# An earlier load of the second full block's list entries, and fixed places for the products of the inverses, in an attention and two expert layers on one core

## The chip, the cores and the metric

One Trainium2 chip (trn2), one of its eight cores. The core has five engines that run their own streams of instructions: TensorE (PE; its weight loads are PEld), VectorE (DVE), ScalarE (ACT), GpSimd (POOL) and SyncE (SP), which here only issues DMAs. They wait for each other through semaphores. An engine also waits on its own semaphore where an instruction reads or overwrites what an earlier one of the same engine wrote or read.

The metric is the time of one execution on the device in microseconds. Before the change three runs took 1020.48, 1023.16 and 1031.33 us, median 1023.16 us.

## The reference

Attention is a recurrence over 768 tokens for 4 x 8 heads of size 40. Its output is 3072 rows of 320 numbers. Two expert layers follow, each sending every row to the one of eight experts with the largest logit:

```
for t in range(S):                                   # S = 768, state 40 x 40 for each head
    y[t]  = r[t] @ state
    Sa    = state @ a[t]
    state = state * w[t] - outer(Sa, b[t]) + outer(v[t], k[t])
x = y as 3072 rows of 320
for layer in (1, 2):                                 # 8 experts, 320 -> 1024 -> 320
    e  = argmax(x @ w_gate (+ modality_bias[modality_id] in layer 2))
    out = softmax weight of e * (relu(x @ w1[e]) @ w2[e])   # rows of expert e only
    x  = out
```

## The kernel before

**Attention** works on 24 chunks of 32 tokens, all 32 heads together, four chunks to a group (groups 0 to 5). Within a chunk the recurrence is written as products of matrices. Its one sequential part is the inverse of a unit lower triangular 32 x 32 matrix for each head and chunk. The four chunks of a group are inverted together: 128 partitions hold one row set each, the matrix in `am`, the growing inverse in `tm` (both are parts of `z_sol` in the trace). `solve` does it by VectorE for groups 2 to 5, in 31 steps s = 0 to 30. Step s forms the product of column s of `am` below the diagonal with row s of `tm` into a scratch tile `pr` (`t1`, line 389), and takes it off the rows of `tm` below s (`t2`, line 395). A step with 64 or more elements and at least two rows is cut by `halves` into two pieces of rows; its four instructions then stand in the order product, product, difference, difference. That holds for steps 2 to 28. Groups 0 and 1 go by the class `Halves`: two 16 x 16 inverses side by side and a join. Its method `rest` (lines 479, 482) finishes the same matrix for the other three chunks, in the same pattern of steps.

The order of all work is written out by hand: `attention` calls the parts of a chunk one after another, and a list of small jobs (`Fill`) is drained between them at set fractions. The steps of the inverses are such jobs, and so are the decay products (lines 201 to 226). On each engine the instructions run in that order. Per chunk the state passes TensorE (`zps`, line 549), VectorE (`zs`, lines 555, 557) and TensorE again (line 523). VectorE also makes `z_ak` (line 363), the attention output `x` (line 1654) and the small steps of routing (lines 965 to 996) there.

**The experts** work on blocks of rows of one expert. `a0` and `b0` are blocks of 228 rows that the layer starts with, `b1` is the first block of 456 rows, and `bs[1]` the second. For a block, `entries` (lines 1238 to 1244) loads its list entries `le`: for each row its place in `x` and its weight. `load1` and `load2` (lines 1198 to 1208) load the first and second weights of its expert into `s1` and `s2`; `conv1` and `conv2` split them into two parts on ScalarE and VectorE. `gather` (line 1249) lets GpSimd fetch the rows that the entries name into `xg`; `split_x` (line 1263) transposes them on TensorE. `block(b, prev, nxt)` runs block b and prepares nxt. It starts with `entries(nxt)` and `load1(nxt)`, and puts `gather(nxt)` behind the first piece of layer 1, `load2(nxt)` behind the last, and the transposes of nxt between the pieces of layer 2. `put` (line 1361) scatters a finished block into `x`. Layer 1 reads its rows from the same `x`, so a gather waits for the last block's scatters. For `b0` the call is `block(b0, a0, b1, begun=True)`: entries, first load and gather of `b1` have been issued ahead of it.

All DMAs of SyncE are issued from one queue in order: an issue that waits holds those behind it.

Of the kernel before, what the change touches and what calls it, by code (L numbers as in the profile page):

```python
# [11 lines left out]
F32 = mybir.dt.float32  # L12
# [4 lines left out]
P = 128  # L17
# [16 lines left out]
FOLD = 18  # L34
FOLDS = (0, 0, 12, 24, 30)
PRES = (0, 0, 7, 15, 15)
TAIL, SPREAD, AHEAD = 42, 60, (80, 91)
WMID, WHALF = 1.4, 0.95
NG = NCH // 4
# [15 lines left out]
def attention(tc, zones, ident, r, k, v, w, a, b, emit_x, hook0, hook1, hook2, hook3, unsafe, extra, tail):  # L55
    nc = tc.nc
    with ExitStack() as ctx:
        cp = ctx.enter_context(tc.tile_pool(name="a_const", bufs=1))
        wp = ctx.enter_context(tc.tile_pool(name="a_work", bufs=2))
# [7 lines left out]
        cut = lambda z, at, *shape: view(zones[z], at, *shape)  # L67
# [300 lines left out]
        def solve(st):  # L368
            box = {}

            def t0():
                box["am"] = am = cut("sol", 0, L, L)
                box["tm"] = tm = cut("sol", L * L, L, L)
                nc.scalar.copy(tm, gtl[:, 3:4].unsqueeze(2).to_broadcast([P, L, L]))
                nc.scalar.copy(tm.rearrange("p t s -> p (t s)")[:, 0 : L * L : L + 1], gtl[:, 2:3].to_broadcast([P, L]))
                nc.vector.transpose(out=am, in_=st["aa"].rearrange("p h c t -> p t (h c)"))

            def halves(s):
                n = L - 1 - s
                if n < 2 or n * (s + 1) < 64:  # L380
                    return [(s + 1, L)]
                return [(s + 1, s + 1 + n // 2), (s + 1 + n // 2, L)]

            def t1(s, a, z):
                am, tm = box["am"], box["tm"]
                if a == s + 1:
                    box["pr"] = wp.tile([P, 256], F32, name="pr", bufs=1)
                prv = box["pr"][:, (a - s - 1) * (s + 1) : (z - s - 1) * (s + 1)].rearrange("p (t j) -> p t j", j=s + 1)
                nc.vector.tensor_mul(prv, am[:, a:z, s : s + 1].to_broadcast([P, z - a, s + 1]),  # L389
                                     tm[:, s : s + 1, : s + 1].to_broadcast([P, z - a, s + 1]))  # L390

            def t2(s, a, z):
                tm = box["tm"]
                prv = box["pr"][:, (a - s - 1) * (s + 1) : (z - s - 1) * (s + 1)].rearrange("p (t j) -> p t j", j=s + 1)
                nc.vector.tensor_sub(tm[:, a:z, : s + 1], tm[:, a:z, : s + 1], prv)

            def t3():
                st["tt"] = tt = wp.tile([P, L, 32], F32, name="tt")
                nc.vector.transpose(out=tt.rearrange("p t u -> p (t u)"), in_=box["tm"].rearrange("p t s -> p (t s)"))

            ops = [t0]
            for s in range(L - 1):
                for f in (t1, t2):
                    for a, z in halves(s):
                        ops.append(lambda f=f, s=s, a=a, z=z: f(s, a, z))
            return ops + [t3]

        class Halves:
# [10 lines left out]
            def ops(self):  # L419
                am, tm, st, n = self.am, self.tm, self.st, L // 2  # L420

                def t0():
                    self.pr = wp.tile([P, 256], F32, name="pr", bufs=1)
                    for o in (0, n):
                        nc.vector.transpose(out=am[:, o : o + n], in_=st["aa"].rearrange("p h c t -> p t (h c)")[:, o : o + n])

                def part(o, s):
                    return self.pr[:, 8 * o : 8 * o + (n - 1 - s) * (s + 1)].rearrange("p (t j) -> p t j", j=s + 1)

                def t1(o, s):  # L430
                    nc.vector.tensor_mul(part(o, s), am[:, o + s + 1 : o + n, o + s : o + s + 1].to_broadcast([P, n - 1 - s, s + 1]),
                                         tm[:, o + s : o + s + 1, o : o + s + 1].to_broadcast([P, n - 1 - s, s + 1]))

                def t2(o, s):
                    x = tm[:, o + s + 1 : o + n, o : o + s + 1]
                    nc.vector.tensor_sub(x, x, part(o, s))

                def t3():
                    self.rows = am[:, :n]
                    st["tt"] = tt = wp.tile([P, L, 32], F32, name="tt")  # L440
                    nc.vector.transpose(out=self.rows, in_=tm.rearrange("p t s -> p s t")[:, :n])
                    for o in (n, 0):
                        nc.vector.transpose(out=tt[:, o : o + n].rearrange("p t u -> p (t u)"), in_=tm[:, o : o + n].rearrange("p t s -> p (t s)"))

                ops = [t0]
                for s in range(n - 1):
                    for f in (t1, t2):
                        for o in (0, n):
                            ops.append(lambda f=f, o=o, s=s: f(o, s))
                return ops + [t3]  # L450
# [699 lines left out]
class Block:  # L1150
    def __init__(self, lay, tab, j, cut=None, first=False, ready=False, own=None):

        self.lay, self.tab, self.j, self.first, self.ready, self.own = lay, tab, j, first, ready, own
        self.cut, self.i = cut or lay.cut, None


class Rows:
# [23 lines left out]
class Experts:  # L1181
# [56 lines left out]
    def entries(self, b):  # L1238
        nc, c = self.nc, b.cut
        self.place(b)  # L1240
        r = nc.values_load(b.tab["reg"][0:1, 2, b.j : b.j + 1], engines=[ET.SP], min_val=0, max_val=LST - c.tb)
        d = nc.sync.dma_start(out=b.le, in_=b.lay.lst[ds(r, c.tb)].rearrange("(h p) w -> p h w", p=c.g))
        if self.loose and not b.lay.route:
            self.lrows.after(d.ins)
# [125 lines left out]
    def block(self, b, prev, nxt, hook=None, begun=False):  # L1370
# [12 lines left out]
                self.place(x)  # L1383
        if nxt is not None:
            if not begun:
                self.entries(nxt)
                self.load1(nxt)
                put(0, lambda: self.gather(nxt))
        for q in range(0 if b.ready else 4):
# [198 lines left out]
def network(tc, r, k, v, w, a, b, moe_w_gate, moe_w1, moe_w2, moe2_modality_id, moe2_w_gate, moe2_modality_bias, moe2_w1, moe2_w2, out):  # L1588
    nc = tc.nc
    with ExitStack() as ctx:  # L1590
# [30 lines left out]
        ex = Experts(tc, wt, ident, rt)  # L1621
# [113 lines left out]
        with ExitStack() as ctx2:  # L1735
# [44 lines left out]
            with tc.manual_schedule():  # L1780
                bs = [b1] + [Block(l1, b1.tab, j) for j in range(1, n1)]
                ex.loose = True
                ex.load1(b1)
                ex.gather(b1)
                for h in range(CUT0.h):
                    ex.put(a0, h)
                ex.block(b0, a0, b1, begun=True)
                prev = b0
                for b_, nxt in zip(bs, bs[1:]):
                    ex.block(b_, prev, nxt)  # L1790
                    prev = b_
                t2 = rt.ahead(tp, 1, CUT2, 2, counts(tp, 1))
                more = [Block(l2, t2, j, first=j == 0) for j in range(2)]
                ex.block(bs[-1], prev, more[0])
                tabs = []
                ex.block(more[0], bs[-1], more[1], lambda: tabs.append(rt.table(tp, 2, CUT2, counts(tp, 2), t2)))
                ex.run(more[1:] + [Block(l2, tabs[0], j) for j in range(n2)])
# [18 lines left out]
```

## Time and profile before

| what | value |
|---|---|
| median of three runs | 1023.16 us (1020.48 to 1031.33) |
| the profiled execution | 1024.33 us, its span 1022.1 us |
| TensorE busy | 906.4 us (89%) |
| VectorE busy | 706.1 us (69%) |
| ScalarE busy | 506.6 us (50%) |
| GpSimd busy | 304.7 us (30%) |
| mean granted clock of TensorE | 0.947 of full speed |

The shares are means over stages with different limits. Attention takes about the first half of the span, the experts the rest, where TensorE is busy for 464 of the 482 us after 540 us. What a row of a view means for one stage has to be read in that stage. The times in a timeline count from the start of the span. A row's idle time in brackets names what ended the wait; "issue" there stands for nothing that the profile shows. A row of a timeline may merge several instructions (x2); its length then runs from the first start to the last end.

### The profile page before, as it was taken

The page shows a single profiled execution, that of the slowest core. Times are in us where ns is not written, and L with a number is a line of the kernel's source. Part 1 is how long each engine was busy: PE and PEld are TensorE (multiplying, and loading weights), DVE is VectorE, ACT ScalarE, POOL GpSimd, SP SyncE. Part 2 cuts the span into 40 slices and gives each one's busy share as a digit, 9 for nine tenths or more (in the row PEclk, how much of TensorE's full clock was granted, in tenths as well). Part 3 has the DMA queues.
Part 4 walks back from the last instruction along what each step waited for, and adds up shares of the span by engine and source line. Part 5 has one row for each costly group of instructions (what it writes and reads, how often), then busy time and mean ns, then how long its engine had stood idle before and what let it go on. Part 6 is the DMA issues. An engine that isn't in the chain of part 4 may idle for free. (4 is left out here: it accounts for less than half of the span.)

```text
span 1022.1 us, 38222 instructions
## 1 busy us (share of the span) xinstructions
PE 906.4 (89%) x16089; PEld 838.8 (82%) x16089; DVE 706.1 (69%) x2022; ACT 506.6 (50%) x991; POOL 304.7 (30%) x361
## 2 busy tenths in 40 slices
PE   7747988788878888988879899999999999999995
PEld 7646777677767777766769799999999999999995
DVE  7799899998996985853545354545464776766762
ACT  6625445445445577643523254444443565665662
POOL 6550021211120211112133334543543433323321
PEclk9779979998999999998989899999999999999998
DMA  5554445433532623226017434445343111271110
GB/s 175 141 136 111 73 107 108 116 90 79 98 86 47 159 51 87 50 51 158 17 28 173 124 97 134 129 106 152 101 126 97 30 40 53 79 214 42 40 41 26
DMA packets 152421, 96.41 MB, mean 94 GB/s; under 512 B 127407, under 2 KB 139585, under 8 KB 151850
## 3 DMA queue, kind: packets, MB, share of 16 engines
q1 hardware_dynamic: 138154, 72.53, 28.3%
q0 software_dynamic: 14080, 21.28, 8.1%
q8 instruction: 130, 2.13, 0.9%
q14 instruction: 57, 0.47, 0.1%
HBM read 112.18 MB, written 14.59 MB: 124 GB/s over the span
## 5 line engine op out<-in xcount | busy, mean ns | idle before, releaser
L1293 PE MATMUL hp<-xs,h 128*128 128x256 f32 (+1 forms) x840 | 157.1, 317 | 0.0
L1304 PE MATMUL yp<-h,hh 128*114 128x320 f32 (+1 forms) x464 | 146.9, 317 | 0.3 <-DMA s<-moe_w 0.3
L1305 PE MATMUL yp<-l,hh 128*114 128x320 f32 (+1 forms) x464 | 144.2, 311 | 0.0
L1306 PE MATMUL yp<-h,hl 128*114 128x320 f32 (+1 forms) x464 | 144.0, 310 | 0.0
L1296 DVE SCALAR_TENSOR_TENSOR hl<-hp,hh 128x456 fp32r<-128x456 f32 (+1 forms) x116 | 76.6, 660 | 90.9 <-ACT hh L1295 90.9
L1293 PEld LDWEIGHTS hp<-xs,h 128*128 128x128 f32 x840 | 124.6, 190 | 3.3
L1295 ACT ACTIVATE hh<-hp 128x456 fp32r<-128x456 f32 (+1 forms) x116 | 66.5, 573 | 110.8 <-PE hp L1293 106.2
L1293 PE MATMUL hp<-xs,l 128*128 128x256 f32 (+1 forms) x504 | 102.5, 312 | 0.0
L1214 DVE TENSOR_TENSOR l<-s,h 128x768 fp32r<-128x768 f32 x88 | 80.6, 956 | 13.1 <-ACT h L1213 10.8
L1304 PEld LDWEIGHTS yp<-h,hh 128*114 128x114 f32 (+1 forms) x464 | 85.3, 184 | 0.6 <-issue 0.5
L1305 PEld LDWEIGHTS yp<-l,hh 128*114 128x114 f32 (+1 forms) x464 | 85.3, 184 | 0.2
L1306 PEld LDWEIGHTS yp<-h,hl 128*114 128x114 f32 (+1 forms) x464 | 85.1, 183 | 0.0
L1293 PEld LDWEIGHTS hp<-xs,l 128*128 128x128 f32 x504 | 80.1, 190 | 3.1
L1249 POOL DMA_INDIRECT xg<-x,le x52 | 61.9, 1190 | 69.2 <-issue 58.0
L1220 DVE TENSOR_TENSOR l<-s,h 128x640 fp32r<-128x640 f32 x88 | 72.6, 825 | 3.0 <-ACT h L1219 3.0
L1361 POOL DMA_INDIRECT out<-yo,ti x28 | 34.5, 1232 | 129.2 <-ACT yo L1357 74.7
L1213 ACT CAST h<-s 128x768 fp32r<-128x768 f32 x88 | 70.4, 835 | 1.6 <-DMA s<-moe_w 1.5
L1219 ACT CAST h<-s 128x640 fp32r<-128x640 f32 x88 | 63.3, 719 | 0.0
L389 DVE TENSOR_TENSOR pr<-z_sol 128x110 f32<-128x110 f32 (+20 forms) x232 | 58.5, 282 | 3.9
L985 POOL TENSOR_TENSOR ccnt<-ccnt,oh 128x8 bf16<-128x8 bf16 x24 | 6.7, 279 | 179.5 <-PE rp L983 145.7
L1003 POOL DMA_INDIRECT lst<-l2e,posi x32 | 40.8, 1276 | 60.9 <-DVE posi L996 53.5
L1267 DVE TENSOR_TENSOR xs<-ta,xs 128x456 fp32r<-128x456 f32 (+1 forms) x28 | 18.5, 662 | 55.2 <-ACT xs L1266 55.2
(364 smaller groups left out, 1996.2 us busy)
## 6 DMA issues: line engine op xcount, KB each, us to landing
s<-moe_w SPq DMA_DIRECT2D x22, 1280.0 KB
s<-moe_w SPq DMA_DIRECT2D x22, 1024.0 KB
s<-moe_w SPq DMA_DIRECT2D x44, 256.0 KB
z_w<-w SPq DMA_DIRECT2D x40, 160.0 KB
z_kb<-k SPq DMA_DIRECT2D x24, 160.0 KB
z_kb<-b SPq DMA_DIRECT2D x24, 160.0 KB
z_pa<-a SPq DMA_DIRECT2D x96, 40.0 KB
rt<-r SPq DMA_DIRECT2D x96, 40.0 KB
```

What stands on the lines that cost most here:

```text
L389: nc.vector.tensor_mul(prv, am[:, a:z, s : s + 1].to_broadcast([P, z - a, s + 1]), tm[:, s : s + 1, : s + 1].to_broadcast([P, z - a, s + 1]))
L1213: nc.scalar.copy(wt["h1"][:, :, s], wt["s1"][:, :, s])
L1214: nc.vector.tensor_sub(wt["l1"][:, :, s], wt["s1"][:, :, s], wt["h1"][:, :, s].bitcast(F32))
L1219: nc.scalar.copy(wt["h2"][:, s], wt["s2"][:, s])
L1220: nc.vector.tensor_sub(wt["l2"][:, s], wt["s2"][:, s], wt["h2"][:, s].bitcast(F32))
L1249: d = self.nc.gpsimd.indirect_dma_start(out=b.xg[:, h], out_offset=None, in_=b.lay.src, in_offset=IndirectOffsetOnAxis(ap=b.le[:, h, 0:1]. ...
L1293: nc.tensor.matmul(out=hp[:, i], lhsT=l, rhs=r, start=k == 0, stop=k == len(ops) - 1)
L1295: nc.scalar.activation(hh[:, s], hp, AF.Relu)
L1296: nc.vector.scalar_tensor_tensor(out=hl[:, s], in0=hp, scalar=0.0, in1=hh[:, s].bitcast(F32), op0=ALU.max, op1=ALU.subtract)
L1304: nc.tensor.matmul(out=yp, lhsT=hh[:, k, t], rhs=wt["h2"][:, k], start=k == 0, stop=False)
L1305: nc.tensor.matmul(out=yp, lhsT=hh[:, k, t], rhs=wt["l2"][:, k], start=False, stop=False)
L1306: nc.tensor.matmul(out=yp, lhsT=hl[:, k, t], rhs=wt["h2"][:, k], start=False, stop=k == 7)
```

## The change

Two things are done.

1. The products of an inverse get fixed places. Before, each step takes a new `pr` tile of 256 numbers (one buffer, so it lies where the last one lay), and the second half's product follows the first half's directly. Now one `pr` tile of 264 numbers is taken at the first step of an inverse; the first half's product, or that of a whole step, lies at 0, the second half's at 128. `Halves` takes the same tile of 264.
2. The list entries of `bs[1]` are loaded ahead of `block(b0, ...)`, and the call of `block` for `b1` doesn't load them again (`listed`).

```diff
+PR = 264
@@ solve
+            def place(s, a, z):
+
+                if "pr" not in box:
+                    box["pr"] = wp.tile([P, PR], F32, name="pr", bufs=1)
+                o = 128 if a > s + 1 else 0
+                return box["pr"][:, o : o + (z - a) * (s + 1)].rearrange("p (t j) -> p t j", j=s + 1)
+
             def t1(s, a, z):
                 am, tm = box["am"], box["tm"]
-                if a == s + 1:
-                    box["pr"] = wp.tile([P, 256], F32, name="pr", bufs=1)
-                prv = box["pr"][:, (a - s - 1) * (s + 1) : (z - s - 1) * (s + 1)].rearrange("p (t j) -> p t j", j=s + 1)
+                prv = place(s, a, z)
                 nc.vector.tensor_mul(prv, am[:, a:z, s : s + 1].to_broadcast([P, z - a, s + 1]),
                                      tm[:, s : s + 1, : s + 1].to_broadcast([P, z - a, s + 1]))
 
             def t2(s, a, z):
                 tm = box["tm"]
-                prv = box["pr"][:, (a - s - 1) * (s + 1) : (z - s - 1) * (s + 1)].rearrange("p (t j) -> p t j", j=s + 1)
+                prv = place(s, a, z)
                 nc.vector.tensor_sub(tm[:, a:z, : s + 1], tm[:, a:z, : s + 1], prv)
@@ class Halves, ops, t0
-                    self.pr = wp.tile([P, 256], F32, name="pr", bufs=1)
+                    self.pr = wp.tile([P, PR], F32, name="pr", bufs=1)
@@ class Block
-        self.cut, self.i = cut or lay.cut, None
+        self.cut, self.i, self.listed = cut or lay.cut, None, False
@@ class Experts, entries
         self.place(b)
+        b.listed = True
@@ class Experts, block
             if not begun:
-                self.entries(nxt)
+                if not nxt.listed:
+                    self.entries(nxt)
                 self.load1(nxt)
@@ network
                 for h in range(CUT0.h):
                     ex.put(a0, h)
+                ex.entries(bs[1])
                 ex.block(b0, a0, b1, begun=True)
```

On VectorE, in the first inverse that the change touches (steps 3 to 5 of group 2), the rows stood so before, with the semaphores that each waits for:

```order
L389 TENSOR_TENSOR pr<-z_sol 128x42 [waits DVE_49]
L389 TENSOR_TENSOR pr<-z_sol 128x45
L395 TENSOR_TENSOR z_sol<-z_sol,pr 128x14x3 [waits DVE_49]
L395 TENSOR_TENSOR z_sol<-z_sol,pr 128x15x3 [waits DVE_49]
L389 TENSOR_TENSOR pr<-z_sol 128x56 [waits DVE_49]
L389 TENSOR_TENSOR pr<-z_sol 128x56
L395 TENSOR_TENSOR z_sol<-z_sol,pr 128x14x4 [waits DVE_49] x2
L389 TENSOR_TENSOR pr<-z_sol 128x65 [waits DVE_49]
L389 TENSOR_TENSOR pr<-z_sol 128x70
```

and so they stand in the changed kernel, the same instructions in the same order:

```order
L395 TENSOR_TENSOR pr<-z_sol 128x42 [waits DVE_49]
L395 TENSOR_TENSOR pr<-z_sol 128x45
L401 TENSOR_TENSOR z_sol<-z_sol,pr 128x14x3 [waits DVE_49]
L401 TENSOR_TENSOR z_sol<-z_sol,pr 128x15x3 [waits DVE_49]
L395 TENSOR_TENSOR pr<-z_sol 128x56 [waits DVE_49] x2
L401 TENSOR_TENSOR z_sol<-z_sol,pr 128x14x4 [waits DVE_49] x2
L395 TENSOR_TENSOR pr<-z_sol 128x65 [waits DVE_49]
L395 TENSOR_TENSOR pr<-z_sol 128x70 [waits DVE_49]
```

Nothing moved; the second product of a step now has a wait of its own. The first product's wait is for another instruction than before: the last difference of the step ahead before (a new tile waits for all that used the old one), now the first difference, which read the place that it overwrites and wrote the row that it reads.

On SyncE, around `block(b0, ...)`, the rows before were these (`s_9408` and `s_9409` are the first and second weights, `le_14741` the entries of `bs[1]`):

```order
L1202 DMA s_9408<-moe_w 128x2x1024
L1204 ISA
L1204 DMA s_9408<-moe_w 64x1024
L1204 ISA
L1204 DMA s_9408<-moe_w 64x1024
L1208 ISA
L1208 DMA s_9409<-moe_w 128x8x320
L1241 TENSOR_LOAD small
L1241 ISA x2
L1242 ISA
L1242 DMA le_14741<-lst_61 114x4x4
```

and they are these in the changed kernel, where the buffers have other numbers:

```order
L1208 DMA s_9288<-moe_w 128x2x1024
L1210 ISA
L1210 DMA s_9288<-moe_w 64x1024
L1210 ISA
L1210 DMA s_9288<-moe_w 64x1024
L1248 TENSOR_LOAD small
L1248 ISA x2
L1249 ISA
L1249 DMA le_14621<-lst_61 114x4x4
L1214 ISA
L1214 DMA s_9289<-moe_w 128x8x320
```

The entries' DMA and the read of its register moved ahead of one DMA, the load of b1's second weights. GpSimd's gathers and scatters stand where they stood.

## Rows read from the trace of the kernel before

**Rows 1.** The profile's page, first line.

```profile
span 1022.1 us, 38222 instructions
```

**Rows 2.** Table by stretch: stretch, length; busy (instructions) of PE, PEld, DVE, ACT, POOL; granted clock.

```profile
184.00:238.00 54.00, 44.70 (x1297) 38.71 (x1298) 51.49 (x177) 21.59 (x49) 8.65 (x11) 0.87 0.39 95
...
249.00:296.00 47.00, 35.03 (x1181) 30.32 (x1180) 45.45 (x134) 20.06 (x45) 7.99 (x9) 0.96 0.52 111
...
345.00:440.00 95.00, 83.70 (x2845) 72.55 (x2846) 72.85 (x288) 63.26 (x137) 14.31 (x20) 0.98 0.37 76
579.00:586.00 7.00, 4.52 (x18) 4.52 (x18) 1.59 (x2) 1.70 (x3) 2.21 (x2) 0.51 0.20 39
```

**Rows 3.** TensorE's waits, 184 to 346 us: for what; total us, times, longest.

```profile
PE rp L982 <- DVE z_ak L363: 6.7, 5, 3.1
PE yps L592 <- DVE x L1654: 5.8, 4, 1.9
...
PE aab L358 <- DVE pr L389: 2.0, 1, 2.0
```

**Rows 4.** TensorE's waits, 346 to 440 us.

```profile
PE zps L549 <- issue: 4.3, 3, 2.4
```

**Rows 5.** VectorE's waits, 184 to 346 us.

```profile
DVE zs L555 <- PE zps L549: 2.7, 2, 2.1
```

**Rows 6.** VectorE's waits, 346 to 440 us.

```profile
DVE zs L555 <- PE zps L549: 5.6, 5, 2.9
```

**Rows 7.** VectorE's timeline, inverses of groups 2 and 5: start us, length us, instruction.

```profile
185.51 0.33 DVE L395 TENSOR_TENSOR z_sol<-z_sol,pr 128x42 f32<-128x42 f32 x2
185.87 0.35 DVE L389 TENSOR_TENSOR pr<-z_sol 128x56 f32<-128x56 f32 x2
186.14 0.34 DVE L395 TENSOR_TENSOR z_sol<-z_sol,pr 128x56 f32<-128x56 f32 x2
186.51 0.37 DVE L389 TENSOR_TENSOR pr<-z_sol 128x65 f32<-128x65 f32 x2
...
436.71 0.22 DVE L389 TENSOR_TENSOR pr<-z_sol 128x60 f32<-128x60 f32 x1
```

**Rows 8.** TensorE's timeline, transposes of bs[1]'s rows.

```profile
581.48 0.45 PE L1263 MATMUL ta<-ident,xg 114*128 114x114 f32 x1 [4.60 <-DMA xg<-x,le]
```

**Rows 9.** GpSimd's timeline, the first gather of bs[1].

```profile
568.07 1.21 POOL L1249 DMA_INDIRECT xg<-x,le x1 [8.14 <-issue]
```

**Rows 10.** Line 1361, 556 to 560 us: who waited for b0's scatter; its landing.

```profile
  POOL xg L1249: 8.1, 1
...
DMA to landing us min/median/max: 8.4/8.6/8.8
```

**Rows 11.** VectorE's timeline, second half of group 1's inverse, fixed places.

```profile
154.73 0.48 DVE L482 TENSOR_TENSOR z_sol<-z_sol,pr 128x128 f32<-128x128 f32 x2
155.13 0.47 DVE L479 TENSOR_TENSOR pr<-z_sol 128x112 f32<-128x112 f32 x2
```

**Rows 12.** Line 389 over the span: count, duration ns min/median/max, first and last start.

```profile
L389 DVE TENSOR_TENSOR pr<-z_sol x232: 158/262/1545, 184.3 to 437.2; 128x110 f32<-128x110 f32 x12, 128x120 f32<-128x120 f32 x12, 128x56 f32<-128x56 f32 x8, 128x78 f32<-128x78 f32 x8
```

**Rows 13.** TensorE's timeline, 232 to 239 us.

```profile
232.11 1.93 PE L358 MATMUL aab<-ab,kT 128*32 128x64 f32 x64 [2.68 <-ACT ab L339]
...
238.32 0.17 PE L982 MATMUL rp<-oh,tri 128*128 128x8 bf16 x1 [0.18 <-DVE z_ak L363]
```

**Rows 14.** ScalarE's timeline, ahead of that copy.

```profile
230.65 0.21 ACT L967 ACTIVATE ex<-dl 128x8 f32<-128x8 f32 x1 [4.51 <-DVE dl L966]
```

**Rows 15.** SyncE's issues around block b0: start us, length us.

```profile
541.18 0.47 SPq L1208 DMA_DIRECT2D s<-moe_w  x1
542.81 0.63 SPq L1242 DMA_DIRECT2D le<-lst  x1
```

**Rows 16.** Line 1242, 542 to 544 us: its waits, ns min/median/max.

```profile
L1242 SPq EVENT_SEMAPHORE  x5: 17/28/28, 542.4 to 542.7; - x5
```

**Rows 17.** ScalarE's timeline, first conversion of b1's second weights.

```profile
559.85 0.72 ACT L1219 CAST h<-s 128x640 fp32r<-128x640 f32 x1
```

## The prediction

> **What bounds the kernel now.** I read the table by stretch first, then the waits of TensorE, then VectorE's timeline inside the inverses, and last the queues around the first blocks of experts.
>
> The profiled execution took 1024.33 us, of which 1022.1 us are its span [rows 1]; the median of the three runs is 1023.16 us, 1.2 us below it. Both parts of the change sit in places of their own, so the table by stretch comes first [rows 2]. From 184 to 238 us VectorE is busy for 51.49 of 54 us, from 249 to 296 us for 45.45 of 47, while TensorE idles 9 and 12 us. From 345 to 440 us it is the other way: TensorE 83.70 of 95 us, VectorE 72.85. All four inverses of groups 2 to 5 run between 184 and 437 us.
>
> Who waits for whom says the same. Between 184 and 346 us TensorE waits for VectorE: 6.7 us for `z_ak`, 5.8 us for `x`, 2.0 us for a product of an inverse itself [rows 3], 14.5 us in these three rows. After 346 us no wait of TensorE names VectorE; the longest, 4.3 us before `zps`, ended by nothing the profile shows [rows 4]. VectorE's waits for `zps` tell which of the two was late at the hand-over of the state: two waits in the first stretch (2.7 us) [rows 5], five in the second (5.6 us) [rows 6]. So VectorE sets the pace up to about 345 us, TensorE after it.
>
> Inside an inverse a step is product, product, difference, difference. The reader is to add start and length of each row [rows 7]. The pair of products at 185.87 ends at 186.22, and the differences that wait for them begin at 186.14: 0.08 us before the end, because each waits for the product one further back. The pair of differences ends at 186.48; the next step's product begins at 186.51, 0.03 us after. It waits for the row directly ahead of it. One such joint thus costs 0.03 + 0.08 = 0.11 us.
>
> In the experts the place of the change is the hand-over from block b0 to b1 to the second full block (bs[1]). TensorE idles 4.60 us before 581.48 us for bs[1]'s gathered rows [rows 8]. The first gather was issued at 568.07 after 8.14 us of idle [rows 9], and that wait was ended by b0's scatter into `x`, which took 8.4 to 8.8 us to land [rows 10].
>
> **The change, part by part.** *Fixed places.* Before, a step's first product gets a new `pr` tile, so it waits for the last difference of the step before, which is the row directly ahead. With fixed places it waits for the difference of its own half, one row further back (that difference also made the row of the inverse it reads). That is the distance at which the differences already overlap by 0.08 us. There is also a row of the trace with the new form: the second half of group 1's inverse keeps its products at fixed places, and there the differences at 154.73 end at 155.21 while the next step's product starts at 155.13, again 0.08 us before [rows 11]. I take 0.11 us for each joint removed; the ends are 0 (the wait is paid anyway) and 0.11.
>
> How many? The 232 products [rows 12] are four inverses of 58: 27 steps in two halves and 4 whole ones. 27 steps of each inverse follow a step with two differences, 108 joints. In VectorE's timeline 93 of them start 0.03 us after the row ahead, the first at 185.87, the last at 436.71 [rows 7]; in the other 15 another job stands between and hides the joint. So VectorE's time falls by at most 93 x 0.11 = 10.2 us.
>
> Not all lies on the path. From 345 us on there are 45 joints; TensorE sets the pace there and does not wait for VectorE [rows 2, 4], so I cost their 5 us at nothing; TensorE's own chain hides them. Of the 48 earlier ones, three lie ahead of a wait of VectorE for `zps` [rows 5]. From 188 to 238 us there are 20, but TensorE's row at 238.32 had waited only 0.18 us for VectorE, and its run up to there began at 232.11 behind a copy of ScalarE that followed VectorE's routing step at 230.45 [rows 13, 14]; only the 15 joints before that move it. From 249 to 296 us there are 13, from 301 to 315 us three, from 325 to 345 us four; the remaining five fall where TensorE runs by itself. On the path: 15 + 13 + 3 + 4 = 35 joints, 35 x 0.11 = 3.9 us.
>
> *Added waits.* The second product of a step now waits too, for the second difference of the step before, with one product between. That is again the distance that shows 0.08 us of overlap [rows 7], so nothing. If that cover failed, 108 x 0.11 = 11.9 us would come back on VectorE and eat the gain. The tile grows by 8 words and is taken once for each inverse: nothing.
>
> *The list entries.* On SyncE's queue the entries of bs[1] go ahead of the load of b1's second weights instead of behind it. Before, the two were issued at 541.18 and 542.81 [rows 15], so they change places: the entries start some 1.6 us earlier and the weights 1.6 us later. The entries' DMA waits for semaphores, with that load and then the load of the next first weights queued behind it on SyncE; its waits in the trace took 17 to 28 ns each [rows 16], so they had been met. Gain: the gather that reads the entries was held by b0's scatter, not by them [rows 9, 10], so 0; the other end is the whole stall of 4.60 us [rows 8]. Loss: the weights were there when ScalarE's first conversion of them began at 559.85 with no idle ahead of it [rows 17]; 1.6 us later they delay it by 0 to 1.6 us. They were issued 18.7 us before that use, so I take 0. What is late next at bs[1] is what was late before: b0's scatter and then the gather.
>
> Sum: 1024.33 - 3.9 - 0 = 1020.4 us for an execution like the profiled one, and 1.2 us less against the median of the runs: **1019.2 us**.
>
> A rule speaks against this. The Trainium skill, VectorE: DVE Perf Modes, section The DRAIN you can't avoid, says that the next operation does not start until the pipeline is empty, and that eight copies took 13.88 us with a semaphore after each or only after the last. By it the sum would be 1024.33. The rows at 186.14 and 155.13 do not agree with it [rows 7, 11]: they begin before the row ahead ends.
>
> **The rivals.** *Handed back.* VectorE finishes sooner and waits for `zps`, `lp` or `yps`. For it: TensorE has gaps that nothing in the profile explains, also before 345 us, and VectorE does wait at times [rows 5]. Against it: 14.5 us of waits for VectorE [rows 3]. Time: 1023.2 us. 15%.
>
> *A joint costs its 0.11 us also without a wait on the row ahead* (the engine empties between jobs, and what I read as overlap is only how ends are recorded). Then nothing is saved: 1023.2 us. The starts themselves speak against it: 0.27 us from a step's first product to its first difference, 0.37 from there to the next step's product, on equal sizes [rows 7]. This is what the Trainium skill's section would give. 4%.
>
> *The entries do gate the gather.* If their landing was as late as the scatter's, the stall of 4.60 us goes, and with it the half clock behind it (0.51 over 7 us [rows 2], 3.4 us): 1019.2 - 8.0 = 1011.2 us. Against it: the wait is put down to the scatter [rows 10]. 6%.
>
> *The clock helps.* Over 184 to 238 us the granted clock is 0.87 [rows 2], so a quarter of the stretch ran at 1.2 GHz, behind gaps in which TensorE waited. Shorter gaps may keep it at 2.4 GHz; half of the 7 us lost there would give 1015.7 us. 13%.
>
> *Slower: the clock falls where TensorE sets the pace.* From 345 to 440 us the grant is 0.98. The gaps there are TensorE's own, and the change shifts everything by some us against transfers and against the clock's changes. Were the stretch granted the 0.87 of 184 to 238 us, TensorE would lose 0.11 x 95 = 10.5 us, and the end would be 1019.2 + 10.5 = 1029.7 us. It decides once more than 3.9 us are lost so. Against it: none of TensorE's gaps there names VectorE [rows 4], so none should grow. 6%.
>
> **How the numbers follow.** The forecast has 56%, for 1017.5 to 1021 us by itself. The range goes down to the clock's help with a little more, 1014.5 us, and up past no change (1023.2) by most of the weights' 1.6 us, 1024.5 us; what is left out is the entries' case and the slower one, and the tails. A measurement of this kernel can tell about 1% from no change, 1012.9 and 1033.4 us here. Faster by more than that needs the entries' case or nearly all 10.2 us: 6%. Slower by more needs the clock's fall and bad luck beside it: 3%. Within 1%: 91%.
>
> **What would show it.** In the inverses no product should start after the end of a difference directly ahead of it, save at the whole steps; VectorE's busy time from 184 to 345 us should fall, and the last inverse end some 4 us or more earlier. The waits of TensorE for `z_ak`, `x` and `pr` should shrink by about 4 us in all. The entries of bs[1] should be issued near 541 us less the shift, the weights behind them, and the gather should still wait for b0's scatter with a stall near 4.6 us. I am wrong if that stall goes, if the saved time turns up as longer waits of VectorE for `zps`, or if the stretch after 345 us becomes longer or shorter than before.

## The result and the profile after

Over 20 runs of each, the changed kernel takes 1010.79 us at the median (999.39 to 1021.25) and the kernel before 1020.36 us (1009.64 to 1031.33). The ratio is 0.9885, with a 95% interval of 0.986 to 0.991, so 9 to 14 us less. (It leaves out the longest runs of both kernels, so it is not quite the ratio of the medians, 0.9906.) The forecast was 1019.2 us. Of the 8.4 us between forecast and result, 2.8 are the base: the three runs shown had a median of 1023.16 us, twenty have 1020.36 us. The other 5.6 us are a gain that the prediction did not see.

The profiled execution took 1012.19 us. The first lines of its page answer to [rows 1]:

```profile
span 1010.0 us, 38222 instructions
PE 901.4 (89%) x16089; PEld 835.4 (83%) x16089; DVE 696.3 (69%) x2022; ACT 507.0 (50%) x991; POOL 305.1 (30%) x361
```

Its table by stretch (columns as in [rows 2], whose stretches it answers to; the last row is new):

```profile
184.00:238.00 54.00, 45.52 (x1419) 39.16 (x1423) 52.23 (x186) 23.39 (x53) 12.61 (x13) 0.94 0.41 98
249.00:296.00 47.00, 37.30 (x1207) 32.04 (x1207) 44.80 (x151) 20.24 (x45) 8.21 (x11) 0.89 0.45 97
341.00:435.00 94.00, 83.71 (x2776) 73.41 (x2776) 66.98 (x277) 61.89 (x133) 14.30 (x20) 0.95 0.39 80
554.00:584.00 30.00, 29.05 (x185) 27.50 (x184) 16.21 (x36) 13.38 (x26) 11.63 (x10) 1.00 0.46 134
```

The same 30 us around the hand-over to bs[1] stood so in the kernel before, some 6 us later in the span:

```profile
560.00:590.00 30.00, 25.40 (x146) 24.00 (x145) 13.19 (x29) 10.50 (x21) 8.98 (x8) 0.89 0.43 125
```

Two places gave the time. VectorE's busy time over the span fell from 706.1 to 696.3 us, and in this pair of traces the last step of an inverse came 5.7 us earlier (next but one fence). One pair does not give the size: in a second trace of each kernel (before_again and change_again, below) that step comes at 433.5 and 431.5 us, 2.0 us apart. And in the 30 us of the hand-over TensorE was busy for 3.7 us more, at full instead of 0.89 of its clock. After that nothing moves any more: the two traces run in parallel, the changed one 11.1 to 12.1 us ahead.

VectorE's timeline in the inverse of group 2, to lay beside [rows 7]:

```profile
186.11 0.34 DVE L395 TENSOR_TENSOR pr<-z_sol 128x56 f32<-128x56 f32 x2
186.37 0.34 DVE L401 TENSOR_TENSOR z_sol<-z_sol,pr 128x56 f32<-128x56 f32 x2
186.62 0.36 DVE L395 TENSOR_TENSOR pr<-z_sol 128x65 f32<-128x65 f32 x2
```

The differences of 186.37 end at 186.71, and the next step's product starts at 186.62, 0.09 us before that end. From product to product the step takes 0.51 us; before it took 0.64 [rows 7]. The joint was worth 0.13 us here; the prediction had 0.11.

The products over the span (columns as in [rows 12]):

```profile
L395 DVE TENSOR_TENSOR pr<-z_sol x232: 172/259/1601, 184.6 to 431.5; 128x110 f32<-128x110 f32 x12, 128x120 f32<-128x120 f32 x12, 128x56 f32<-128x56 f32 x8, 128x78 f32<-128x78 f32 x8
```

At the hand-over, the timeline of GpSimd, SyncE and TensorE in the changed kernel (L1368 is the scatter, L1256 the gather, L1214 the load of second weights):

```profile
537.34 0.32 SPq L1249 DMA_DIRECT2D le<-lst  x1
538.02 0.83 SPq L1214 DMA_DIRECT2D s<-moe_w  x1
...
552.41 0.39 SPq L1208 DMA_DIRECT2D s<-moe_w  x1
...
561.83 1.21 POOL L1256 DMA_INDIRECT xg<-x,le  x1 [7.02 <-issue]
...
566.36 1.20 POOL L1256 DMA_INDIRECT xg<-x,le  x1 [0.30 <-issue]
567.24 0.38 SPq L1214 DMA_DIRECT2D s<-moe_w  x1
...
571.88 0.32 PE L1270 MATMUL ta<-ident,xg 114*128 114x114 f32 x1 [0.95 <-DMA xg<-x,le]
```

The wait of 4.60 us [rows 8] has become 0.95 us. b0's scatters, the last thing ahead of the gather, landed sooner after their issue than in [rows 10]:

```profile
DMA to landing us min/median/max: 7.2/7.3/7.4
```

The same timeline of the kernel before shows what the prediction looked past. The last of the four gathers was issued only 0.57 us ahead of bs[1]'s second weights, and it took over 8.8 us until TensorE had its rows at 581.48:

```profile
557.54 0.38 SPq L1202 DMA_DIRECT2D s<-moe_w  x1
...
572.59 1.60 POOL L1249 DMA_INDIRECT xg<-x,le  x1 [0.30 <-issue]
573.16 0.38 SPq L1208 DMA_DIRECT2D s<-moe_w  x1
```

In the changed kernel this lead is 0.88 us, and the rows are there 5.5 us after the issue. The first weights of bs[1] at 552.41 and 557.54 let the distances be compared: from there to the first gather it is 9.42 us now and was 10.53 us before. From there to bs[1]'s second weights it is 14.83 us now and was 15.62 us before, which is why the lead grew by less than the gather gained.

### The profile page after: what moved, and what is told of

Read it like the earlier page. It is cut to its first block, busy times and chain, and to the rows that moved or that the text cites. A ratio compares the mean times of both kernels' runs of the same rounds, so it can differ in the third digit from the quotient of the medians.

```text
span 1010.0 us, 38222 instructions
## 1 busy us (share of the span) xinstructions
PE 901.4 (89%) x16089; PEld 835.4 (83%) x16089; DVE 696.3 (69%) x2022; ACT 507.0 (50%) x991; POOL 305.1 (30%) x361
## 5 line engine op out<-in xcount | busy, mean ns | idle before, releaser
L1256 POOL DMA_INDIRECT xg<-x,le x52 | 60.9, 1171 | 68.2 <-issue 58.6
L1368 POOL DMA_INDIRECT out<-yo,ti x28 | 33.9, 1211 | 129.9 <-ACT yo L1364 74.7
L401 DVE TENSOR_TENSOR z_sol<-z_sol,pr 128x110 f32<-128x110 f32 (+20 forms) x232 | 54.6, 267 | 0.5
L395 DVE TENSOR_TENSOR pr<-z_sol 128x110 f32<-128x110 f32 (+20 forms) x232 | 53.5, 260 | 0.7
```

The costliest lines, as they stand in the source:

```text
L1256: d = self.nc.gpsimd.indirect_dma_start(out=b.xg[:, h], out_offset=None, in_=b.lay.src, in_offset=IndirectOffsetOnAxis(ap=b.le[:, h, 0:1]. ...
```

## The experiments

All times are against the kernel before, run beside each on the same chip. A ratio is the time over that of the kernel before. The lead is the time from the issue of the last of bs[1]'s four gathers to that of bs[1]'s second weights; it is negative where the weights were issued first.

| kernel | ratio (95%) | lead of the last gather over bs[1]'s second weights, us | TensorE's wait for the rows, us | first weights of bs[1] to first gather, us |
|---|---|---|---|---|
| before, first trace | | 0.57 | 4.60 | 10.53 |
| before_again | one run | 0.95 | none | 10.15 |
| fixed_only | 0.9961 (0.992 to 1.0002) | 0.24 | 3.72 | 10.86 |
| fixed_early | 0.9947 (0.9914 to 0.9979) | 0.90 | 0.33 | 10.20 |
| fixed_late | 1.001 (0.9973 to 1.0047) | 0.22 | 4.29 | 10.88 |
| serial_halves | 1.0033 (0.9993 to 1.0073) | -0.47 | 4.04 | 10.95 |
| scratch_ahead | 0.9961 (0.9923 to 0.9999) | -0.45 | 5.03 | 10.97 |
| entries_only | 0.9972 (0.9929 to 1.0016) | 1.06 | 0.45 | 9.42 |
| entries_first | 0.9955 (0.9914 to 0.9996) | 1.06 | 0.22 | 9.45 |
| entries_twice | 0.9951 (0.9917 to 0.9985) | 1.73 | none | 9.38 |
| weights_late | 0.9962 (0.9925 to 0.9999) | 1.07 | 0.16 | 9.40 |
| weights_behind_gather | 0.9949 (0.9913 to 0.9984) | 5.18 | none | 10.85 |
| fixed_and_hold | 0.9919 (0.9881 to 0.9956) | 5.06 | none | 9.86 |
| the change | 0.9885 (0.986 to 0.991) | 0.88 | 0.95 | 9.42 |
| change_again | 0.9843 (0.979 to 0.9895) | 1.06 | none | 9.43 |
| change_and_hold | 0.9869 (0.9819 to 0.9918) | 5.63 | none | 9.67 |

The last three columns are read from the timelines of GpSimd, SyncE and TensorE of each profiled execution, as in the fences here. Over all sixteen traces the wait goes by the lead: with 0.57 us or less it is 3.7 to 5.0 us, with 0.88 us or more it is under 1 us.

**Fixed places alone (fixed_only).**

```diff
-                ex.entries(bs[1])
                 ex.block(b0, a0, b1, begun=True)
```

> Only the fixed places; the entries of bs[1] stay behind the load of b1's second weights. Of the 11.5 us that the change gained, the two traces put 5 to 6 us before 560 us and 6 us into the stretch from there to 595 us. Theory A (the joints give the first part, the order on SyncE's queue the second): 4 to 6 us faster than before (ratio 0.994 to 0.996), TensorE's wait of over 3 us for bs[1]'s gathered rows still there. Rival B (the second part only comes from everything arriving some 5 us earlier against the transfers): about 11 us faster (0.989), and that wait under 1.5 us. The prediction as written: 3.9 us.

4 us faster by the ratio, and TensorE's wait stood there: theory A. The interval runs from 8 us less to no change, so the size is confirmed only roughly. The rows of the wait, in the timeline of fixed_only:

```profile
566.51 1.28 POOL L1256 DMA_INDIRECT xg<-x,le  x1 [0.30 <-issue]
566.75 0.38 SPq L1214 DMA_DIRECT2D s<-moe_w  x1
...
574.19 0.45 PE L1270 MATMUL ta<-ident,xg 114*128 114x114 f32 x1 [3.72 <-DMA xg<-x,le]
```

**Which joints count (fixed_early, fixed_late).** Groups 2 and 3, or groups 4 and 5, keep their products at fixed places; the others take a new tile for each step as before.

```diff
-            def place(s, a, z):
+            def place(s, a, z, new=False):
...
-                o = 128 if a > s + 1 else 0
+                if "pr" not in box or new and not fixed and a == s + 1:
+                    box["pr"] = wp.tile([P, PR], F32, name="pr", bufs=1)
+                o = 128 * (a > s + 1) if fixed else (a - s - 1) * (s + 1)
...
-            ops = solve(st)
+            ops = solve(st, ga in FIXED)
```

> Fixed places in the inverses of groups 2 and 3 alone, up to about 315 us; the entries as before. With the path as in the prediction: about 3.5 us faster (0.9965), nearly all that fixed_only gives. If the place of a joint does not matter: half of what fixed_only gives, about 2 us.

> Fixed places in the inverses of groups 4 and 5 alone, from about 325 us on, the entries as before. If only what VectorE does before 345 us is on the path, as the prediction has it: 0 to 1 us faster, though VectorE's busy time there falls by about 5 us. If every joint counts: about 5 us faster (0.995).

VectorE's busy time falls about alike in both: from 706.1 to 701.4 us with the early inverses and to 700.3 us with the late ones. The time falls only with the early ones, by 5.4 us (2.1 to 8.7), and not with the late ones, 1.0 us more (2.8 less to 4.8 more). In the whole change the late joints show up again as waits of VectorE. Its waits for `yps` and `zps`, first in the kernel before from 346 to 440 us (the second row is [rows 6]), then in the changed one from 341 to 435 us:

```profile
DVE x L1654 <- PE yps L602: 4.1, 3, 3.4
```

```profile
DVE x L1662 <- PE yps L608: 8.2, 4, 4.4
DVE zs L561 <- PE zps L555: 6.1, 3, 4.0
```

14.3 us against 9.7: nearly all of the 5 us that VectorE saves there it waits. It holds over all sixteen traces: in the 94 us that end 3 us after the start of the last product, these two waits come to 12.5 to 15.5 us in the six traces with fixed places in the late inverses, and to 7.3 to 9.7 us in the ten without. The size of fixed_early is not clean: its trace happens to have no long wait at bs[1] either.

**More joints (serial_halves).** Each half's product is followed at once by its difference.

```diff
-                for f in (t1, t2):
-                    for a, z in halves(s):
+                for a, z in halves(s):
+                    for f in (t1, t2):
                         ops.append(lambda f=f, s=s, a=a, z=z: f(s, a, z))
```

> Fixed places, but each half's product is followed at once by its own difference, so that two joints of every step stand bare (216 in four inverses) in place of 108 before and none with the change; entries as before. VectorE's busy time grows by at most 25 us against the change, 12.6 us against before. If 35 of 93 joints lie on the path, as the prediction has it: 4 to 6 us slower than before (1.004 to 1.006). If every joint counts: 12 us slower (1.012). If joints cost nothing: no change.

3.4 us slower than before (0.7 less to 7.4 more), 7.4 us slower than fixed_only by the two ratios. Inside the inverses the rows are what the prediction's joint says:

```profile
185.11 0.21 DVE L395 TENSOR_TENSOR pr<-z_sol 128x42 f32<-128x42 f32 x1
185.35 0.20 DVE L401 TENSOR_TENSOR z_sol<-z_sol,pr 128x42 f32<-128x42 f32 x1
185.47 0.20 DVE L395 TENSOR_TENSOR pr<-z_sol 128x45 f32<-128x45 f32 x1
185.71 0.21 DVE L401 TENSOR_TENSOR z_sol<-z_sol,pr 128x45 f32<-128x45 f32 x1
```

A difference that waits for the row directly ahead starts 0.03 us after its end (185.35 after 185.32), the product behind it, which doesn't, 0.08 us before the end (185.47, 185.55). VectorE's busy time is 710.7 us, 15.0 us more than the 695.7 us of fixed_only; of a joint only the 0.08 us of lost overlap counts as busy, so 216 joints would be 17.3 us. 216 joints of 0.11 us are 23.8 us; 7.4 us of them in the time is 31%, near the 35 of 93 (38%) that the prediction put on the path. The two intervals together would allow anything from a fifth to nearly twice the 7.4 us, so the share is confirmed only roughly.

**The entries alone (entries_only).**

```diff
+                ex.entries(bs[1])
                 ex.block(b0, a0, b1, begun=True)
```

`listed` is as in the change.

> Only the entries of bs[1] ahead of the load of b1's second weights; the inverses as before. Theory A: 5 to 7 us faster (0.993 to 0.995), the last gather of b1 landing without TensorE waiting for it, and the wait for bs[1]'s rows under 1.5 us. Rival B and the prediction as written: no change (0.999 to 1.001), the wait for bs[1]'s rows near 4.6 us.

The wait for bs[1]'s rows is 0.45 us, as theory A has it. By itself that proves little, since one of the two traces of the unchanged kernel has no wait either (before_again). What speaks against B is the distance from the first weights to the first gather: 9.42 us, against 10.53 and 10.15 us in those two. By the ratio it is 2.9 us faster, which its interval (7.3 less to 1.6 more) tells neither from no change nor from the low end of the 5 to 7 expected. The scatter's and the gather's times fit the whole change (9.42 us in the last column).

**Entries early, or weights late (entries_first, entries_twice, scratch_ahead, weights_late).** Moving the entries does two things: they come earlier, and b1's second weights start later.

```diff
entries_first:
+                ex.entries(bs[1])
                 ex.load1(b1)
                 ex.gather(b1)
entries_twice: as entries_only, and block() still loads them
scratch_ahead:
+                scr = tp.tile([114, 4, 4], F32, name="scr")
+                nc.sync.dma_start(out=scr, in_=l1.lst[0:456].rearrange("(h p) w -> p h w", p=114))
                 ex.block(b0, a0, b1, begun=True)
weights_late:
+                scr = tp.tile([1, 4, 4], F32, name="scr")
+                for i in range(4):
+                    nc.sync.dma_start(out=scr[:, i], in_=l1.lst[i : i + 1])
                 ex.block(b0, a0, b1, begun=True)
```

> Inverses as before; the entries of bs[1] still earlier, ahead of both weight loads of b1, so that the second weights follow the first ones directly as before. If the gain is that the entries themselves come sooner: as entries_only, 5 to 7 us faster. If it is that the second weights start later than b1's last gather: the gather lands late again as before and the gain is gone or halved, 0 to 3 us. By the prediction: no change.

> Inverses as before. The entries of bs[1] are loaded twice, ahead of the load of b1's second weights and once more behind it. In the traces so far b0's scatters land 7.2 us after their issue where the entries go ahead of those weights, 8.4 to 8.7 us where they go behind them, and the gather and TensorE's wait follow. If it counts that the entries are there early or that the weights start later: the scatters land in about 7.2 us and TensorE's wait for bs[1]'s rows is under 1.5 us, as in entries_only. If it counts that a small load with many pieces stands on the queue right ahead of the first weights of bs[1]: 8.4 to 8.7 us and a wait of 3.7 to 4.6 us, as before, and no gain.

> Inverses and entries as before; a load of 456 other list rows, of the same shape as the entries of bs[1], into a tile that nobody reads goes ahead of the load of b1's second weights. If what speeds up b0's scatters is only that a load with many small pieces, or a later start, stands ahead of these weights: the scatters land in about 7.2 us, TensorE's wait for bs[1]'s rows is under 1.5 us, and the time is 5 us under before (0.995). If it is that the entries themselves no longer stand between b1's second weights and bs[1]'s first ones: 8.4 to 8.7 us, a wait of about 4 us, and the time of before.

> Inverses and entries as before; four loads of one list row each, into a tile that nobody reads, go ahead of the load of b1's second weights, so that these start some 2 us later, as with the change. If their later start is what counts: b0's scatters land in about 7.2 us, the last gather of bs[1] is issued over 0.8 us ahead of bs[1]'s second weights, TensorE's wait for these rows is under 1.5 us, and the time is 3 to 6 us under before (0.994 to 0.997). If the entries themselves have to be early: 8.4 to 8.7 us, a wait of about 4 us and the time of before.

entries_first removed the wait, but there the entries held both weight loads of b1 behind them: the second ones start 13.6 us ahead of bs[1]'s first, later still than with the change, so it did not part the two. entries_twice shows that nothing is wrong with a small load behind b1's second weights. weights_late parts them: the entries come late, even at 544.66 us, and the first gather still follows the first weights after 9.40 us, where the unchanged kernel on the same chip took 10.15 us (before_again). The lead is 1.07 us and the wait 0.16 us, which alone would not tell, since before_again has none. It is 3.9 us faster (0.1 to 7.6).

```profile
537.80 1.14 SPq L1789 DMA_DIRECT2D scr<-lst  x4
539.28 0.41 SPq L1208 DMA_DIRECT2D s<-moe_w  x1
...
544.66 0.33 SPq L1242 DMA_DIRECT2D le<-lst  x1
...
553.32 0.41 SPq L1202 DMA_DIRECT2D s<-moe_w  x1
...
567.88 1.19 POOL L1249 DMA_INDIRECT xg<-x,le  x1 [0.30 <-issue]
568.95 0.40 SPq L1208 DMA_DIRECT2D s<-moe_w  x1
...
572.83 0.32 PE L1263 MATMUL ta<-ident,xg 114*128 114x114 f32 x1 [0.16 <-DMA xg<-x,le]
```

Here b1's second weights start 14.0 us ahead of bs[1]'s first ones. In every trace with 13.6 to 14.5 us the first gather follows at 9.4 to 9.7 us, with 15.0 us or more at 9.86 to 11.0 us. Within either group the gather does not go by the distance. By this reading scratch_ahead delayed them too little (15.0 us), and its trace has the wait; that the switch lies between 14.5 and 15.0 us rests on this one trace, since the next ones are at 15.3 us and more:

```profile
549.12 0.75 SPq L1208 DMA_DIRECT2D s<-moe_w  x1
...
564.14 0.40 SPq L1202 DMA_DIRECT2D s<-moe_w  x1
...
575.11 1.81 POOL L1249 DMA_INDIRECT xg<-x,le  x1 [8.59 <-issue]
...
588.74 0.45 PE L1263 MATMUL ta<-ident,xg 114*128 114x114 f32 x1 [5.03 <-DMA xg<-x,le]
```

Its ratio is nevertheless 0.9961, 4.0 us faster, with an interval that all but reaches no change. The execution in the trace took 1031.17 us, the longest of its twelve (median 1020.67 us); whether the others had the wait is not known, so the ratio speaks neither for nor against this reading.

**The wait itself (weights_behind_gather).**

```diff
         if nxt is not None:
+            if nxt.hold is not None:
+                self.nc.sync.dma_start(out=nxt.hold, in_=nxt.xg[0:1, nxt.cut.h - 1, 0:4])
             self.load2(nxt)
...
+                bs[1].hold = tp.tile([1, 4], F32, name="hold")
                 ex.block(b0, a0, b1, begun=True)
```

> Inverses and entries as before; the load of bs[1]'s second weights gets a small copy of the last gathered row ahead of it on SyncE's queue, so that it starts only when bs[1]'s gather has landed. If the gather's last piece was late because these weights started 0.2 to 0.6 us behind it: it lands in about 4 us, TensorE's wait of 3.7 to 4.6 us is gone with the half clock behind it, and the time is 5 to 7 us under before (0.993 to 0.995), as entries_only. If the weights are then late for the next block, the gain is given back there. If the wait has another cause, the wait stays and the time is that of before.

5.2 us faster (1.6 to 8.8) and no wait, though the first gather came as late as before (10.85 us): what the stall hangs on is the order of the last gather and bs[1]'s second weights. Nothing was given back later: from the first gather of bs[1] to the end of the span it takes 445.7 us, against 446.4 us in the trace of the unchanged kernel without the wait and 454.0 us in the one with it.

**Do the parts add up (fixed_and_hold, change_and_hold, change_again).** The same hold in the kernel with fixed places alone, in the whole change, and the change once more.

> Fixed places, the entries as before, and bs[1]'s second weights held behind the landing of its gather. If the wait for bs[1]'s rows is all that the moved entries give: as the whole change, 9 to 13 us under before (0.987 to 0.991). If the entries give something else beside it: 4 to 7 us (0.993 to 0.996).

> The whole change, and bs[1]'s second weights held behind the landing of its gather as in weights_behind_gather. If the order of the last gather and these weights is what the stall hangs on: no wait for bs[1]'s rows at all, and 0 to 2 us under the changed kernel (0.987 to 0.989 of before), since its profiled execution still waited 0.95 us. If the two remedies add up as if independent: 5 us more (0.984).

> The changed kernel once more on the chip of the two others, for comparison with them: 9 to 13 us under before (0.987 to 0.991), TensorE's wait for bs[1]'s rows under 1.5 us, b0's scatters landing in 7.2 us. If the wait was absent from its first profile by chance, it may come back here with 8.4 us.

fixed_and_hold gains 8.2 us (4.5 to 12). That lies between its two forecasts, and the interval holds both, so it does not decide whether the moved entries give something else beside the missing wait. The hold adds nothing to the change (0.9869 and 0.9843, the intervals overlap), as expected where the wait is short already. No version beats the changed kernel beyond these intervals. change_again gave more than expected, 16 us (11 to 21).

The traces together give the two sizes better than one pair. From the start of the first product of the four inverses to that of the last it takes 247.9 to 254.8 us in the eight traces with the inverses as before (mean 251.2 us) and 242.6 to 248.7 us in the five with fixed places in all four groups (mean 246.7 us): 4.5 us. From the first gather of bs[1] to the end of the span it takes 451.0 to 454.0 us in the five traces with the long wait (mean 452.4 us) and 445.0 to 449.5 us in the eleven others (mean 447.1 us): 5.2 us for an execution that has the wait.

**Is the wait there each time (before_again)?**

> The kernel before once more. If the wait for bs[1]'s rows is a property of its order: 3.7 to 5 us again, with the last gather issued less than 0.6 us ahead of bs[1]'s second weights or behind their issue. If it is chance: under 1.5 us.

Chance, in part: this trace of the unchanged kernel has a lead of 0.95 us and no wait (its one run took 1013.97 us). Of the seven traces in which b1's second weights start early and nothing is held, five have the long wait; of the six in which they start late, none has it (0.95 us at most).

## Why the prediction was wrong

**Right: the inverses.** The cost of a joint was 0.11 us predicted and 0.11 to 0.13 us in the rows. VectorE's busy time is 695.2 to 696.3 us in the five traces with fixed places in all four groups and 703.8 to 706.1 in the eight with the inverses as before, 9 us between the means, against at most 10.2 us predicted. Late joints at nothing: fixed_late and VectorE's longer waits. 3.9 us on the path: fixed_only's 4 us, within a wide interval, and the 4.5 us between the means of the traces. TensorE's waits for VectorE from 184 to 341 us shrank by less than the 4 us forecast, from 14.5 us [rows 3] to 11.9 us:

```profile
PE rp L988 <- DVE z_ak L364: 6.0, 5, 2.2
PE yps L598 <- DVE x L1662: 4.4, 4, 2.2
...
PE aab L359 <- DVE pr L395: 1.5, 1, 1.5
```

The rival *The clock helps* stays untested. From 184 to 238 us the granted clock was 0.94 in the changed kernel's trace, against 0.87 before, as that rival has it; but a second trace of the unchanged kernel has 0.93 there, so the rise cannot be put down to the change, and no run parts it from the joints. (The 4.3 us that the prediction calls the longest wait before `zps` are three waits together, the longest 2.4 us [rows 4]; nothing hangs on it.)

**The rule against it.** The Trainium skill, VectorE: DVE Perf Modes, section The DRAIN you can't avoid, reports eight copies that took the same time with a semaphore after each and after the last only; by that, taking away waits between VectorE's operations would have given nothing. The same section also says that a next operation that is not held starts earlier, which the prediction left out. For these operations of 0.2 us the traces do not agree with the first: 0.11 to 0.13 us for each joint.

**Wrong: the entries at nothing.** The step reads: "the gather that reads the entries was held by b0's scatter, not by them [rows 9, 10], so 0", and for the weights that make way, "they delay it by 0 to 1.6 us ... I take 0". The first half is true, and it is not the question: weights_late gains with the entries left behind. I priced the move for those who wait for the two loads, not for those who share the transfers with them. With the later weights b0's scatters land sooner (7.3 us after their issue, against 8.6 and 7.9 us in the two traces of the kernel before), the gather follows, and its last piece gets far enough ahead of bs[1]'s second weights. "What is late next at bs[1] is what was late before" failed there. So the 0 us for the entries measured 2.9 us by the ratio of entries_only, in a wide interval, and 5.2 us between the traces with the wait and those without. With the wait of 3.7 to 5.0 us goes the half clock behind it [rows 2]; from 568.07 us on, the traces drift apart by a further 5.4 us, from 6.2 to 11.6.

The prediction took the 4.60 us [rows 8] for a fixed length. It gave the whole stall's end 6%, and for another reason, that the entries land late; its 1011.2 us lies near the result by luck. The mechanism was another. The 3.4 us for the half clock are worked out over 7 us of which TensorE still waited 2.5 us; the rows of TensorE behind the wait (from 581.48 us on) follow each other at 0.27 us up to 586.0 us and at 0.15 us from there, so the half clock cost some 2 us:

```profile
585.47 0.47 PE L1306 MATMUL yp<-h,hl 128*114 128x320 f32 x1
...
586.15 0.31 PE L1306 MATMUL yp<-h,hl 128*114 128x320 f32 x1
586.30 0.31 PE L1304 MATMUL yp<-h,hh 128*114 128x320 f32 x1
```

And its base was 2.8 us too high. The rows to see it by were there: the last gather at 572.59, 0.57 us ahead of a load at 573.16, with its rows 8.9 us later, where the first two gathers had landed 4.1 us after their issue. A wait that hangs on who comes first by half a microsecond can go or come by a shift of 1 us; moving a load by 1.6 us is such a shift.

**What stays open.** Why b0's scatters land sooner when b1's second weights start 2 us later, although these are done before: in the 1.4 us ahead of bs[1]'s first weights the DMA engines are busy for 0.06 of the time in both traces (556.0 to 557.4 us before, 550.9 to 552.3 us after). The landing goes with it in every trace that shows it (7.2 to 7.8 us against 7.7 to 8.8 us), but the step between was not shown. And the parts: some 4 to 5 us for the fixed places and 3 to 5 us for the hand-over by the ratios, against 9 to 14 us for the whole. By the traces they are 4.5 and 5.2 us, but the kernel before does not have the wait in every execution, and how often is not known; the intervals leave room for the rest, and do not settle it.

## What to carry to other kernels

When a load is moved on a queue, list not only who waits for it but which other transfers run in the time that it leaves and the time that it enters, and how close the next race is. A stall whose length is set by which of two transfers is issued first is not a term to carry over at its old length: it has two values, and one trace shows one of them. Nor does one pair of traces give the size of a part: the two traces of the unchanged kernel differ by 3.7 us at the last step of the inverses (437.2 and 433.5 us). For a chain of short operations on VectorE, such as these of 0.2 us, putting one independent instruction between writer and reader is worth 0.11 to 0.13 us a joint, but only where VectorE sets the pace.

## What the hardware showed that was not expected

The last piece of a gather is all or nothing against a weight load of 1280 KB: issued 0.88 us or more ahead of it, its rows were there within 5.5 us (566.36 to 571.88); issued 0.57 us ahead, after 8.9 us (572.59 to 581.48); 0.24 us ahead, after 7.7 us (566.51 to 574.19). Over all traces it is at most 5.5 us with 0.88 us or more, and 7.7 to 8.9 us, in no order, with 0.57 us or less. The Trainium skill, DMA: Bandwidth & Descriptors, section Queues, rings and completion order, says that a DMA engine takes turns between its queues packet by packet; so a piece that is issued well ahead would meet fewer of these turns. The traces agree in the direction between these two groups, and show a step rather than a slope; how the turns fell was not seen.

A scatter of b0 (two pieces of 114 rows) took 7.2 to 7.8 us to land beside the first weights of bs[1] (1024 KB and twice 256 KB) where b1's second weights, already finished, had been issued 13.8 to 14.4 us ahead of these, and 7.7 to 8.8 us where it was 15.3 to 16.4 us.
